# Silu in one ScalarE step for half of the gates, and the last tiles cut in column halves

## The chip, the cores and the metric

One core of a Trainium2 chip runs the kernel. The time is the device time of one execution in microseconds (us), and a median over several executions is quoted. Each execution also has a profiled span, from the first to the last instruction that the profile records. Ratios are computed as the mean time of one kernel's runs over that of the other's in the same rounds, so they are not quite the ratio of the quoted medians.

## The reference, cut to what matters

```python
x = A_x                                       # 2048 rows of 512
xn = _layernorm(x)
s = _A_ref(xn, A_wqkv, A_wo)                  # dilated local attention, then @ wo
g = _silu(_B_ref(xn, B_w1, B_w2, B_w3, B_w4)) # mixer and MLP: x1 + gelu(norm(x1) @ w3) @ w4
return x + s * g
```

The end of the kernel is `x + s * silu(x1 + h2)`: for each tile of 128 rows, the last MLP product (w4), the gate, the output projection (wo), a product, an add and a store.

## The kernel before: the parts that matter

Rows are split by parity: p is 0 for even rows and 1 for odd ones, with eight tiles each. Tiles t = 8 to 15 of the MLP are those of parity 1. `final_tile(p, i)` makes output tile i of parity p.

```python
    def w4_tile(t):
        ...
        def half(lo, hi):                       # lo..hi: part of the 11 steps of the contraction
            if lo == 0:
                st["pt"] = psb("w4_ps")
            pt = st["pt"]
            for ft in range(lo, hi):            # L521: TensorE
                nc.tensor.matmul(pt, lhsT=h3(c, ft, 1)[...], rhs=w4_sb[:fs, ft, :], ...)
            if hi == NF:
                x_i = xn[p][:, i, :]            # L527: VectorE
                nc.vector.tensor_tensor(out=x_i, in0=pt, in1=x_i, op=ALU.add)

    def gate(t):                                # x_i becomes 2 * silu(x_i)
        ...
        nc.scalar.activation(sig, x_i, AF.Tanh, scale=0.5)                        # L536: ScalarE
        nc.vector.scalar_tensor_tensor(out=x_i, in0=sig, scalar=1.0, in1=x_i,
                                       op0=ALU.add, op1=ALU.mult)                 # L537: VectorE

    def final_tile(p, i, eng=nc.vector, ps=psb, act=False):
        ...                                     # L683: four matmuls with wo
        if act:
            nc.scalar.copy(out=sg, in_=pt)                                        # L690
        nc.vector.tensor_tensor(out=sg, in0=sg if act else pt, in1=xn[p][:, i, :], op=ALU.mult)  # L691
        eng.tensor_tensor(out=x_o, in0=sg, in1=x_o, op=ALU.add)                   # L693

    ...                                         # the end of the program:
    for t in range(8, 16):
        w4s[t](4 * (t == 8), NF)
        if t == 10:
            normalise_end(1, 1)
        if t == 13:
            normalise_end(1, 2)                 # L660, L665: needs the last reciprocal denominators
        if t < 15:
            p, i = fq.pop(0)                    # (0,6), (1,0), (1,1), ... (1,5)
            final_tile(p, i, ps=psa)
            gate(t)
            ...                                 # stores
        if t == 10:
            normalise_mid(1, 2)                 # the reciprocal, and its way out to memory
            normalise_rr(1, 2)                  # and back, broadcast
    final_tile(0, 7, ps=psa)
    store(nc.sync, 0, 7, 1)
    gate(15)
    final_tile(1, 6, ps=psa, act=True)
    store(nc.sync, 1, 6, 1)
    final_tile(1, 7, ps=psa)
    store(nc.scalar, 1, 7, 1)
```

The factor 2 in the gate is paid back by attention denominators that are doubled (a column of 2.0 in the values).

The softmax here doesn't subtract the row's maximum and nothing guards it: scores larger than these inputs give would overflow.

Of the kernel before, what the change touches and what calls it, by code (L numbers as in the profile page):

```python
# [8 lines left out]
AF = mybir.ActivationFunctionType  # L9
ALU = mybir.AluOpType  # L10
# [5 lines left out]
def kernel(  # L16
# [14 lines left out]
    nc = tc.nc  # L31
    P = 128
    S = 2048
    D = 512
# [4 lines left out]
    ND = D // P  # L39
    NF = (F + P - 1) // P  # L40
# [43 lines left out]
    def at(kb, n, m):  # L84
        ar, o = (arenas[0], int(kb * KB)) if kb < 170 else (arenas[1], int((kb - 176) * KB))
        return ar[:, o : o + n * m].rearrange("p (n m) -> p n m", n=n)

    xn = [at(8 * p, M // P, D) for p in range(2)]
# [15 lines left out]
    oT = [at(176, ND, M), at(B0 + 17, ND, X)]  # L104
# [4 lines left out]
    w4_sb = at(121.5, NF, D)  # L109
    wo_sb = at(62, ND, D)  # L110
    xo = [at(B0 + 25.5, M // P, D), at(67, M // P, D)]
# [12 lines left out]
    def psb(name):  # L124
        cnt["b"] += 1
        return pst("wb"[cnt["b"] % 2], name)[:, 0, :]

    wqkv_v = A_wqkv.rearrange("(dt q) n -> q dt n", q=P)
    for c in range(NCH):
        p, k = c // 2, c % 2  # L130
        n = 1 if c == 0 else 2
        for t0 in range(k * TPC, (k + 1) * TPC, n):
            nc.sync.dma_start(
                out=xn[p][:, t0 : t0 + n, :],
                in_=xv[p, t0 * P : (t0 + n) * P, :].rearrange("(i q) d -> q i d", q=P),
# [354 lines left out]
    def h3(c, ft, n):  # L490
        if c < 3:
            return h3T[c][:, ft : ft + n, :]
        return h3T_lo[:, ft : ft + n, :] if ft < 8 else h3T_hi[:, ft - 8 : ft - 8 + n, :]
# [16 lines left out]
    def w4_tile(t):  # L510
        c, jj = t // TPC, t % TPC
        p, i = c // 2, (c % 2) * TPC + jj
        st = {}

        def half(lo, hi):
            if lo == 0:
                st["pt"] = psb("w4_ps")
            pt = st["pt"]
            for ft in range(lo, hi):
                fs = P if ft < NF - 1 else FL  # L520
                nc.tensor.matmul(  # L521
                    pt, lhsT=h3(c, ft, 1)[:fs, 0, jj * P : (jj + 1) * P], rhs=w4_sb[:fs, ft, :],
                    start=(ft == 0), stop=(ft == NF - 1),
                )
            if hi == NF:
                x_i = xn[p][:, i, :]
                nc.vector.tensor_tensor(out=x_i, in0=pt, in1=x_i, op=ALU.add)  # L527

        return half

    def gate(t):
        c, jj = t // TPC, t % TPC
        p, i = c // 2, (c % 2) * TPC + jj
        x_i = xn[p][:, i, :]
        sig = fin.tile([P, D], BF16, name="sig", tag="f")
        nc.scalar.activation(sig, x_i, AF.Tanh, scale=0.5)  # L536
        nc.vector.scalar_tensor_tensor(out=x_i, in0=sig, scalar=1.0, in1=x_i, op0=ALU.add, op1=ALU.mult)  # L537
# [83 lines left out]
    def normalise_dn(p, r):  # L621
        n = H * runs[p][r][3] // P
        dn = small.tile([P, n], BF16, name="dn", tag="dn")
        nc.sync.dma_start(out=dn, in_=rrs[p, r][0].rearrange("h (a m) -> (h a) m", a=P // 8))
        rrs[p, r][0] = dn
# [11 lines left out]
    def normalise_mid(p, r):  # L637
        _, _, ra, rw = runs[p][r]
        n = H * rw // P
        dn, rden_d = rrs[p, r]  # L640
        rb = small.tile([P, n], BF16, name="rb", tag="rb")
        with nc.allow_low_precision("bf16 weights"):
            nc.vector.reciprocal(out=rb, in_=dn)
        nc.sync.dma_start(out=rden_d.rearrange("h (a m) -> (h a) m", a=P // 8), in_=rb)

    def normalise_rr(p, r):
        _, _, ra, rw = runs[p][r]
        dn, rden_d = rrs[p, r]
        if p == 0 and r:
            rr = orws[r % 2][:, 0 : ND * rw]  # L650
        else:
            rr = at(rr_at[r % 2] if p else B0 + 8, 1, ND * rw)[:, 0, :]
        nc.sync.dma_start(out=rr, in_=rden_d.unsqueeze(1).to_broadcast([8, DH, ND * rw]))
        rrs[p, r] = rr

    def normalise_end(p, r):
        _, _, ra, rw = runs[p][r]
        rr = rrs[p, r].rearrange("p (s q) -> p s q", s=ND)
        n = min(rw, M - ra)
        nc.vector.tensor_tensor(  # L660
            out=oT[p][:, :, ra : ra + n], in0=oT[p][:, :, ra : ra + n], in1=rr[:, :, 0:n], op=ALU.mult
        )
        if rw > n:
            a = M - DW + W
            nc.vector.tensor_tensor(  # L665
                out=oT[0][:, :, a:M], in0=oT[p][:, :, a + DW : X], in1=rr[:, :, a + DW - ra : rw], op=ALU.mult
            )
# [7 lines left out]
            in_=xv[p, 4 * k * P : (4 * k + 4) * P, :].rearrange("(i q) d -> q i d", q=P),  # L675
        )

    def final_tile(p, i, eng=nc.vector, ps=psb, act=False):
        pt = ps("wo_ps")
        if ps is psa:  # L680
            pt = pt[:, 0, :]
        for dt in range(ND):
            nc.tensor.matmul(  # L683
                pt, lhsT=oT[p][:, dt, i * P : (i + 1) * P], rhs=wo_sb[:, dt, :],
                start=(dt == 0), stop=(dt == ND - 1),
            )
        cnt["g"] += 1
        sg = at(sg_at[cnt["g"] % 3], 1, D)[:, 0, :]
        if act:
            nc.scalar.copy(out=sg, in_=pt)  # L690
        nc.vector.tensor_tensor(out=sg, in0=sg if act else pt, in1=xn[p][:, i, :], op=ALU.mult)  # L691
        x_o = xo[p][:, i, :]
        eng.tensor_tensor(out=x_o, in0=sg, in1=x_o, op=ALU.add)  # L693

    def store(q, p, i, n=2):
        q.dma_start(
            out=ov[p, i * P : (i + n) * P, :].rearrange("(i q) d -> q i d", q=P), in_=xo[p][:, i : i + n, :]
        )
# [118 lines left out]
    w4s = [w4_tile(t) for t in range(S // P)]  # L817
# [3 lines left out]
    for k in range(NU):  # L821
        a, b = groups[N1 + k]
        gates = [lambda t=t: gate(t) for t in ready]
        ready = fill.get(k, ())
        if ready:
            a += gates
            if len(ready) == 2:
                a.append(lambda t=ready[0]: w4s[t](0, NF))
                late[N1 + k].append(lambda t=ready[0]: gate(t))
                ready = ready[1:]  # L830
            t = ready[-1]
            a.append(lambda t=t: w4s[t](0, 6))
            b.append(lambda t=t: w4s[t](6, NF))
        else:
            i0, i1, i2 = rows_of[k]
            a.append(lambda i=i0: final_tile(0, i, nc.gpsimd))
            a.append(lambda i=i1: final_tile(0, i, nc.gpsimd))
            a += gates
            b.append(lambda i=i2: final_tile(0, i, nc.gpsimd))
# [77 lines left out]
    pack(1, 2)  # L917
    normalise_dn(1, 2)
    gate(7)
    for i in (0, 2, 4):  # L920
        store(nc.sync, 0, i)
    fq = [(0, 6)] + [(1, i) for i in range(6)]
    for t in range(8, 16):
        w4s[t](4 * (t == 8), NF)
        if t == 10:
            normalise_end(1, 1)
        if t == 13:
            normalise_end(1, 2)
        if t < 15:
            p, i = fq.pop(0)  # L930
            final_tile(p, i, ps=psa)
            gate(t)
            if p == 0:
                store(nc.sync, p, i, 1)
            elif i % 2:
                store(nc.sync, p, i - 1)
        if t == 10:
            normalise_mid(1, 2)
            normalise_rr(1, 2)
    final_tile(0, 7, ps=psa)  # L940
    store(nc.sync, 0, 7, 1)
    gate(15)
    final_tile(1, 6, ps=psa, act=True)
    store(nc.sync, 1, 6, 1)
    final_tile(1, 7, ps=psa)
    store(nc.scalar, 1, 7, 1)


# [28 lines left out]
```

## Time and profile before

| | before |
|---|---|
| time, median of 3 | 206.06 us |
| profiled span | 204.1 us |
| TensorE's last result | 199.11 us |
| VectorE's last add ends | 201.03 us |
| last store issued | 201.06 us |

The median and the profile come from different executions: the profiled one took 205.92 us. The prediction shows the lines behind the last three rows.

### The profile page before, as it was taken

How to read it: one execution, taken by the hardware profiler on the slowest of the kernel's cores; microseconds unless marked ns; L12 is line 12 of the kernel's file. 1: busy time of each engine (PE TensorE's matmuls, PEld its weight loads, DVE VectorE, ACT ScalarE, POOL GpSimd, SP SyncE). 2: the span in 40 equal slices, each digit the busy share in tenths (PEclk: the TensorE clock that was granted, in tenths of full speed). 3: DMA queues.
4: the chain of work that ended last, by engine and by line, in shares of the span. 5: the costliest groups of instructions: out<-in, count | busy, mean ns of one | idle time of the engine just before them, and what ended most of it. 6: DMA issues, size and time to landing. Idle time of an engine off the chain costs nothing.

```text
span 204.1 us, 4800 instructions
## 1 busy us (share of the span) xinstructions
PE 195.2 (96%) x1900; PEld 94.9 (47%) x1928; DVE 135.0 (66%) x256; ACT 131.5 (64%) x157; POOL 74.5 (37%) x149
## 2 busy tenths in 40 slices
PE   7899999999999999999999999999999999999990
PEld 2585445444444444444444444444555444444440
DVE  5788897626298988856930101288577968888693
ACT  2366768657988888896556657898788877212130
POOL 5889842100023095964691000003830590700000
PEclk9999999999999999999999999999999999999997
DMA  5992264577900089495798948794220241553312
GB/s 146 356 348 80 87 139 86 85 109 112 275 34 5 14 199 140 75 254 107 181 196 184 295 148 136 109 278 156 36 51 5 56 89 26 116 165 118 117 51 77
DMA packets 33197, 26.74 MB, mean 131 GB/s; under 512 B 14600, under 2 KB 31088, under 8 KB 33176
## 3 DMA queue, kind: packets, MB, share of 16 engines
q1 hardware_dynamic: 30984, 23.22, 44.8%
q0 software_dynamic: 2048, 3.09, 8.9%
q8 instruction: 15, 0.25, 0.5%
q10 hardware_dynamic: 144, 0.13, 0.2%
q14 instruction: 6, 0.05, 0.1%
HBM read 12.40 MB, written 4.98 MB: 85 GB/s over the span
## 4 chain that ended last, share of the span: by engine, by line
PE 71%; DVE 11%; DMA 9%; issue 3%; POOL 3%; ACT 2%; SPq 0%; DVEq 0%; POOLq 0%
PE w_ps L501 19%; PE w_ps L521 10%; PE v_ps L547 8%; PE s_ps L567 7%; PE w_ps L457 6%; PE qk_ps L401 5%; PE w_ps L434 5%; PE o_ps L590 4%; PE qk_ps L419 4%; DMA den_d<-orw 3%; PE wo_ps L683 3%; DMA arena<-rden_d 2%; DVE arena L537 2%; DMA rden_d<-rb 1%; DVE arena L691 1%
## 5 line engine op out<-in xcount | busy, mean ns | idle before, releaser
L572 ACT ACTIVATE arena<-s_ps 128x960 bf16<-128x960 f32 (+1 forms) x68 | 62.7, 975 | 13.7 <-PE s_ps L567 13.7
L521 PE MATMUL w_ps<-arena 128*128 128x512 bf16 (+1 forms) x156 | 38.5, 380 | 0.6 <-issue 0.2
L506 ACT ACTIVATE arena<-w_ps 128x1024 bf16<-128x1024 f32 x20 | 20.5, 1024 | 14.5 <-PE w_ps L501 13.1
L632 POOL DMA_DIRECT2D arena<-orw x48 | 25.0, 528 | 5.8 <-DVE orw L602 5.8
L501 PEld LDWEIGHTS <-arena 128*128 128x128 bf16 (+1 forms) x176 | 17.5, 100 | 20.5 <-issue 0.4
L521 PEld LDWEIGHTS <-arena 128*128 128x128 bf16 (+1 forms) x176 | 16.5, 98 | 19.5
L693 POOL TENSOR_TENSOR arena<-arena 128x512 bf16<-128x512 bf16 x6 | 7.7, 1302 | 44.4 <-DVE arena L691 44.4
L536 ACT ACTIVATE sig<-arena 128x512 bf16<-128x512 bf16 x16 | 10.1, 631 | 21.0 <-DVE arena L527 20.9
L551 DVE CAST v_aug<-v_ps 128x512 bf16<-128x512 f32 x17 | 11.7, 690 | 15.4 <-PE v_ps L547 15.3
L602 DVE CAST orw<-o_ps 128x960 bf16<-128x960 f32 (+1 forms) x17 | 19.7, 1156 | 3.1 <-PE o_ps L590 3.0
L401 PE MATMUL qk_ps<-arena 128*128 128x512 bf16 (+1 forms) x109 | 20.4, 332 | 0.5 <-ACT arena L321 0.3
L501 PE MATMUL w_ps<-arena 128*128 128x512 bf16 (+1 forms) x86 | 19.4, 379 | 0.2
L501 PE MATMUL w_ps<-arena,arena 128*128 128x512 bf16 (+1 forms) x86 | 19.1, 379 | 0.1
L547 PE MATMUL v_ps<-wv_sb,arena 128*128 128x512 bf16 x67 | 17.5, 380 | 0.1
L567 PEld LDWEIGHTS <-arena 32*128 32x128 bf16 x544 | 10.2, 92 | 14.8 <-issue 14.7
L567 PE MATMUL s_ps<-arena 32*128 32x120 bf16 (+1 forms) x544 | 16.1, 213 | 0.1
L527 DVE TENSOR_TENSOR arena<-w_ps,arena 128x512 bf16<-128x512 f32 x16 | 11.0, 686 | 7.9 <-PE w_ps L521 7.9
L273 POOL TENSOR_SCALAR l3r<-l3m 128x1 f32<-128x1 f32 (+1 forms) x10 | 2.4, 238 | 37.6 <-DVE l3m L282 37.6
L457 PE MATMUL w_ps<-arena 128*128 128x512 bf16 x63 | 15.2, 380 | 0.1
L660 DVE TENSOR_TENSOR arena<-arena,orw 128x1440 bf16<-128x1440 bf16 (+1 forms) x2 | 1.6, 783 | 19.8 <-DMA orw<-rden_d 19.8
L434 PE MATMUL w_ps<-arena 128*128 128x512 bf16 x63 | 14.6, 379 | 0.0
L401 PEld LDWEIGHTS <-arena 128*128 128x128 bf16 x112 | 10.6, 98 | 7.9 <-DMA arena<-in_A_wqkv_dram 0.8
(99 smaller groups left out, 273.4 us busy)
## 6 DMA issues: line engine op xcount, KB each, us to landing
x1n_dram<-arena SPq DMA_DIRECT2D x5, 512.0 KB, 3.0
arena<-in_A_x_dram SPq DMA_DIRECT2D x4, 512.0 KB, 6.1
arena<-in_A_x_dram SPq DMA_DIRECT2D x6, 256.0 KB, 6.6
out_dram<-arena SPq DMA_DIRECT2D x6, 256.0 KB, 3.6
arena<-in_B_w_dram SPq DMA_DIRECT2D x1, 1376.0 KB
arena<-in_B_w_dram SPq DMA_DIRECT2D x1, 1280.0 KB
arena<-arena SPq DMA_DIRECT2D x16, 72.0 KB, 2.6
arena<-arena SPq DMA_DIRECT2D x16, 68.0 KB, 4.0
```

Source lines behind the costliest of these rows:

```text
L401: nc.tensor.matmul(pt[:, b, hh * w : (hh + 1) * w], lhsT=wqk_sb[:, dt, nt * P : (nt + 1) * P], rhs=xnT[p][:, dt, k * CH + hh * w : k * CH ...
L434: nc.tensor.matmul(pt[:, b, :], lhsT=w1_sb[:, dt, g * P : (g + 1) * P], rhs=xn2T[c][:, dt, :], start=(dt == 0), stop=(dt == ND - 1),)
L457: nc.tensor.matmul(pt, lhsT=w2_src(p, g, m0), rhs=w2_sb[:, g, :], start=(g == 0), stop=(g == ND - 1))
L501: nc.tensor.matmul(pt[:fs, ft % 2, :], lhsT=w3_sb[:, dt, ft * P : ft * P + fs], rhs=x1nT[c][:, dt, :], start=(dt == 0), stop=(dt == ND - 1),)
L506: nc.scalar.activation(h3(c, 2 * a, 2), pt, AF.Gelu_apprx_tanh)
L521: nc.tensor.matmul(pt, lhsT=h3(c, ft, 1)[:fs, 0, jj * P : (jj + 1) * P], rhs=w4_sb[:fs, ft, :], start=(ft == 0), stop=(ft == NF - 1),)
L547: nc.tensor.matmul(vp[:nk, :], lhsT=xnT[p][:, dt, k0 : k0 + nk], rhs=wv_sb[:, dt, :], start=(dt == 0), stop=(dt == ND - 1),)
L551: nc.vector.tensor_copy(out=va[:nk, :, 0:DH], in_=vp[:nk, :].rearrange("p (h d) -> p h d", d=DH))
L567: nc.tensor.matmul(st[:nk, b, i * nq : (i + 1) * nq], lhsT=kT[e][r : r + 32, dt, k0 : k0 + nk], rhs=qT[e][r : r + 32, dt, q0 : q0 + nq], s ...
L572: nc.scalar.activation(prv[:nk, 2 * h : 2 * h + 2], st[:nk, :, 0 : 4 * nq], AF.Exp, scale=SCALE)
L602: nc.vector.tensor_copy(out=orw[p, r][:, :, :, q0 - ra : q0 - ra + nq], in_=op[:, :, 0 : 4 * nq].rearrange("p j (s q) -> p j s q", q=nq),)
L632: nc.gpsimd.dma_start(out=oT[p][DH * hh : DH * (hh + 1), :, ra : ra + rw], in_=orw[p, r][32 * cg : 32 * cg + DH, jj],)
```

## The change

Its intent is to take VectorE's load off the tail. The gates of parity 1 become one Silu on ScalarE, in place. The output product doubles what is now a plain silu. The last MLP tile is made in two column halves, one behind the final of (0,7) and one behind that of (1,6), so that its gate lies beside TensorE's work. The last output tile is made in two halves too.

```diff
-        def half(lo, hi):
+        def half(lo, hi, ds=slice(0, D)):           # all of pt, w4_sb and x_i cut to columns ds
...
-    def gate(t):
+    def gate(t, ds=slice(0, D)):
...
+        if p:
+            nc.scalar.activation(x_i, x_i, AF.Silu)
+            return
...
-        if act:
-            nc.scalar.copy(out=sg, in_=pt)
...
+        for lo in range(0, D, n):                   # n = D // halves; matmuls, product, add per half
+            if p:
+                nc.vector.scalar_tensor_tensor(
+                    out=sg[:, ds], in0=pt, scalar=2.0, in1=x_i[:, ds], op0=ALU.mult, op1=ALU.mult
+                )
...
     gate(7)
+    nc.scalar.preload_act_table_set("silu_and_others")
...
     final_tile(0, 7, ps=psa)
     store(nc.sync, 0, 7, 1)
-    gate(15)
-    final_tile(1, 6, ps=psa, act=True)
+    w4s[15](0, NF, halves[0])                       # was whole, ahead of the final of (0,7)
+    gate(15, halves[0])
+    final_tile(1, 6, ps=psa)
     store(nc.sync, 1, 6, 1)
-    final_tile(1, 7, ps=psa)
+    w4s[15](0, NF, halves[1])
+    gate(15, halves[1])
+    final_tile(1, 7, ps=psa, halves=2)
     store(nc.scalar, 1, 7, 1)
```

## The prediction

> **What bounds the kernel now.** I read the page first, then the chain of waits for the last 38 us, then VectorE and TensorE one by one in order of time, then a table of busy time by stretch. The page says TensorE is busy 96% of the span, so outside the tail only less TensorE work could help, and the change removes none.
>
> ```profile
> PE 195.2 (96%) x1900; PEld 94.9 (47%) x1928; DVE 135.0 (66%) x256; ACT 131.5 (64%) x157; POOL 74.5 (37%) x149
> ...
> PE 71%; DVE 11%; DMA 9%; issue 3%; POOL 3%; ACT 2%; SPq 0%; DVEq 0%; POOLq 0%
> ```
>
> The end is different. TensorE's last instructions in order of time (start, us, engine, line, operation):
>
> ```profile
> 193.98 1.89 PE L521 MATMUL w_ps<-arena 128*128 128x512 bf16 x8
> 195.71 0.81 PE L521 MATMUL w_ps<-arena,arena 128*128 128x512 bf16 x3
> 196.36 1.03 PE L683 MATMUL wo_ps<-arena,arena 128*128 128x512 bf16 x4
> 197.22 1.89 PE L683 MATMUL wo_ps<-arena 128*128 128x512 bf16 x8
> ```
>
> The reader sees the last MLP tile (L521, eleven matmuls), then the finals of (0,7), (1,6), (1,7), without a gap, the last result at 197.22 + 1.89 = 199.11. VectorE from there back:
>
> ```profile
> 190.08 0.69 DVE L527 TENSOR_TENSOR arena<-w_ps,arena 128x512 bf16<-128x512 f32 x1 [0.62 <-PE w_ps L521]
> 191.94 0.78 DVE L660 TENSOR_TENSOR arena<-arena,arena 128x1184 bf16<-128x1184 bf16 x1 [1.17 <-DMA arena<-rden_d]
> 192.63 0.27 DVE L665 TENSOR_TENSOR arena<-arena,arena 128x224 bf16<-128x224 bf16 x1
> ...
> 196.74 0.68 DVE L527 TENSOR_TENSOR arena<-w_ps,arena 128x512 bf16<-128x512 f32 x1
> 197.43 0.69 DVE L691 TENSOR_TENSOR arena<-wo_ps,arena 128x512 bf16<-128x512 f32 x1
> 198.15 0.43 DVE L693 TENSOR_TENSOR arena<-arena 128x512 bf16<-128x512 bf16 x1
> 198.49 0.68 DVE L537 SCALAR_TENSOR_TENSOR arena<-sig,arena 128x512 bf16<-128x512 bf16 x1
> 199.10 0.42 DVE L691 TENSOR_TENSOR arena<-arena 128x512 bf16<-128x512 bf16 x1
> 199.55 0.42 DVE L693 TENSOR_TENSOR arena<-arena 128x512 bf16<-128x512 bf16 x1
> 199.89 0.68 DVE L691 TENSOR_TENSOR arena<-wo_ps,arena 128x512 bf16<-128x512 f32 x1
> 200.61 0.42 DVE L693 TENSOR_TENSOR arena<-arena 128x512 bf16<-128x512 bf16 x1
> ```
>
> Up to 190.8 VectorE waits 0.5 to 0.6 us for TensorE in every tile (the bracket of the first line). At 190.77 it waits 1.17 us for a transfer, the reciprocal denominators. From 191.94 it never waits again: it is behind, and it ends at 201.03, 1.92 us after TensorE. The store is issued at 201.06 and the span ends at 204.1, a fixed 3.04 us. So only the 1.92 us between TensorE's and VectorE's ends can be won.
>
> **What the Trainium skill says.** "ScalarE: Activation LUTs", section "Table sets: the hidden batching unit", lists exp and tanh in one set, and "What ACT_TABLE_LOAD costs" gives 1283 ns for a load, with a drain 2.66 us, and the same time per element for every function. The trace agrees on the load: four of 1.28 us, none after 127.2 since exp and tanh share it; a drain is not seen (the ACTIVATE follows at 128.50, 0.01 us after the load):
>
> ```profile
> 127.21 1.28 ACT L572 ACT_TABLE_LOAD   x1
> 128.50 1.94 ACT L572 ACTIVATE arena<-s_ps 128x1024 bf16<-128x1024 f32 x2
> ```
>
> "TensorE: Matmul & The Clock Gate", section "Back-to-back issue gap", gives 518 cycles for 512 columns and 262 for 256, so halving columns should double the count at nearly no cost. The trace agrees: the chain has 16 matmuls of 256 columns in 1.75 us (0.109 each), and 49 of 512 in 10.74 (0.219). "VectorE: DVE Perf Modes", section "The perf-mode tier table", puts a bf16 tensor_tensor from SBUF at twice the rate of one with a PSUM operand; here 0.425 against 0.686 us. No table line there has scalar_tensor_tensor; the trace has 0.684 us for it even in bf16 from SBUF, so I take 0.69 for the new one that reads PSUM.
>
> **The change, part by part.**
> 1. Silu gates, tiles 8 to 15. Removed from VectorE: eight L537 of 0.68 us, which cost 0.60 each from start to start, 4.8 us in all. On ScalarE a Tanh of 0.63 becomes a Silu of 0.63 (estimate: same width, same engine). The product of L691 becomes a scalar_tensor_tensor of the same length (the factor 2 balances the doubled denominators). For tiles 8 to 13 the 4.8 us are not on the path: VectorE only waits longer for TensorE. Only the gates of 14 and 15, in the backlog, count.
> 2. One table load more, after gate 7. ScalarE ends that Tanh at 172.20 and gets the next gate at 174.71: 2.51 us idle. 1.28 us fits; 2.66 would just about fit too, and Silu 8 is first used by the product at 178.0. Cost 0.
> 3. Gate 10 leaves VectorE ahead of the reciprocal (183.44), which feeds the denominators. The stage's transfers can start up to 0.6 us earlier, and L660 with them, at 191.4 instead of 191.94.
> 4. Order at the end of TensorE: before, tile 15 then (0,7), (1,6), (1,7). After: (0,7), half of 15, (1,6), other half of 15, (1,7) in two halves. The order of instructions of the built program confirms it. The columns are the same: PE still ends at about 199.1, plus 0.03 us for 30 matmuls more.
> 5. The copy of (1,6) on ScalarE (0.59) goes, and its product reads PSUM: +0.26 us of VectorE (0.68 for 0.42).
> 6. Halves on VectorE. Estimates of 256 columns: casts of 512 and 960 columns from PSUM take 0.690 and 1.148, so 1.02 ns a column and 0.17 fixed, hence 0.43; bf16 adds of 224 and 512 take 0.27 and 0.425, hence 0.285; Silu from ACT copies of 128, 512 and 1024 (0.27, 0.59, 1.02), 0.83 ns a column, hence 0.42.
>
> Walk through the new tail, with 0.04 us from producer to consumer and 0.08 overlap between independent VectorE instructions, both as in the lines above. TensorE results: (1,5) 194.15, (0,7) 195.01, 15 first half 196.20, (1,6) 197.07, 15 second half 198.25, (1,7) halves 198.69 and 199.15. VectorE: L660 191.4, L665 to 192.3, product and add of (1,4) to 193.4, tile 14 to 194.06, (1,5) to 195.3, (0,7) to 196.4, tile 15 first half to 196.74; here it has caught up and waits for (1,6): 197.11 to 198.25; second half 198.29 to 198.71; Silu on ScalarE 198.80 to 199.22; (1,7) first product 198.73 to 199.15, its add to 199.46, second product 199.40 to 199.82, its add to 200.12. So VectorE ends at about 200.15 in place of 201.03: **0.9 us** won, 206.06 - 0.9 = 205.2. A check of the sum: the same instructions packed without waits lose two gates (1.2), gain 0.26 and four small extra starts of about 0.15; the rest of the backlog goes into waits for TensorE.
>
> **The rivals.**
> (a) All 4.8 us are won (about 201.3). Against it: the 0.5 to 0.6 us waits for TensorE in front of L527 in each tile, and PE at 3.24 us per tile with no gap. It cannot be, unless TensorE got faster.
> (b) The Silu becomes the last wait: it stands between L527 and the last product. My slack is 0.2 us at the last half, 2 us and more at others. If the small ops cost 0.2 more each, 205.5.
> (c) The denominators come late all the same, since stores of (1,0) are queued in front of the write (the table by stretch shows the transfer engines 56% busy at 180 to 187). Then L660 begins at 191.9, VectorE catches up only at (1,6); the end is the same within 0.1. If it came 0.4 us later than before, TensorE's (1,5), which starts at 193.12 with L660 ending at 192.72, would be held, and the time would be 205.5 to 206.
> (d) The table load is placed badly or drains long, holding gate 8: nothing waits before 178.0, so 205.2 still.
>
> **Range and chances.** The ceiling of gain: last TensorE result 199.15, then a half product and a half add, 0.04 + 0.43 + 0.04 + 0.285, gives 199.95, a gain of 1.1; to this the runs' own spread of 0.3. The floor: rival (b) or (c), a gain of 0.3. So 204.7 to 205.9, and 205.2 in the middle. 2% is 4.1 us, twice what lies after TensorE's end; so within 2% is all but certain, 0.98; faster 0.01, slower 0.01.
>
> **What will show it.** Right: VectorE waiting for TensorE (not for a transfer or nothing) at (1,6) near 197.1; VectorE's last add ending near 200.1, TensorE's last result near 199.15, end 3.04 us after; one table load after 172.2 with ScalarE idle around it; VectorE busy about 4.7 us less on the page (8 x 0.684 removed, 0.26 for part 5 and some 0.49 for the halves added). Wrong: a TensorE gap in the last 10 us, a Silu longer than 0.63, products from PSUM longer than 0.69, 256-column instructions that don't shrink to 0.43 and 0.285, or a wait for the Silu in front of the last product. Had TensorE's end moved by more than 0.1 us, my whole sum would be off.

## The result, and the profile after

The changed kernel took 205.78 us (median of 6, 205.69 to 205.89) against 206.13 us for the kernel before (median of 6), a ratio of 0.9982 with a 95% interval of 0.9969 to 0.9995. The gain is 0.35 us, less than half of the 0.9 that was forecast.

The profile shows a gain twice as large. (In the lines, `w_ps` and `wo_ps` are the PSUM tiles that TensorE writes for w4 and wo, `arena` is the large on-chip tile in which the kernel lays out most of its data, and `rden_d` is the memory buffer through which the reciprocal denominators go.) This is the first line of the changed kernel's page; before it read 204.1 us.

```profile
span 203.4 us, 4821 instructions
```

VectorE in order of time in the changed kernel (start, us, engine, line, operation, and in brackets the idle time and what ended it):

```profile
190.23 0.69 DVE L527 TENSOR_TENSOR arena<-w_ps,arena 128x512 bf16<-128x512 f32 x1 [1.16 <-PE w_ps L521]
192.24 0.78 DVE L663 TENSOR_TENSOR arena<-arena,arena 128x1184 bf16<-128x1184 bf16 x1 [1.32 <-DMA arena<-rden_d]
...
196.90 0.42 DVE L527 TENSOR_TENSOR arena<-w_ps,arena 128x256 bf16<-128x256 f32 x1
197.34 0.69 DVE L696 SCALAR_TENSOR_TENSOR arena<-wo_ps,arena 128x512 bf16<-128x512 f32 x1
198.07 0.42 DVE L701 TENSOR_TENSOR arena<-arena 128x512 bf16<-128x512 bf16 x1
198.48 0.42 DVE L527 TENSOR_TENSOR arena<-w_ps,arena 128x256 bf16<-128x256 f32 x1
198.99 0.42 DVE L696 SCALAR_TENSOR_TENSOR arena<-wo_ps,arena 128x256 bf16<-128x256 f32 x1
199.44 0.29 DVE L701 TENSOR_TENSOR arena<-arena 128x256 bf16<-128x256 bf16 x1
199.65 0.42 DVE L696 SCALAR_TENSOR_TENSOR arena<-wo_ps,arena 128x256 bf16<-128x256 f32 x1
200.10 0.29 DVE L701 TENSOR_TENSOR arena<-arena 128x256 bf16<-128x256 bf16 x1
```

Three things are to be seen. In the middle tiles VectorE's idle time in front of L527 has nearly doubled, from 0.62 to 1.16 us: there the removed gates bought nothing. L663 (L660 before) still waits for the denominators, longer than before (1.32 us against 1.17). And the last add ends at 200.39, where it ended at 201.03. This trace also starts its work later: the same matmul of the tail stands at 172.53, before at 172.37, because the first input landed 0.16 us later (VectorE's first statistics start at 2.97, before at 2.81). Without that, VectorE's tail is 0.80 us shorter.

TensorE and ScalarE in the changed kernel:

```profile
197.94 0.49 PE L521 MATMUL w_ps<-arena,arena 128*128 128x256 bf16 x3
198.28 1.04 PE L691 MATMUL wo_ps<-arena 128*128 128x256 bf16 x8
```

```profile
172.38 1.28 ACT L928 ACT_TABLE_LOAD   x1
174.81 0.63 ACT L536 ACTIVATE arena<-arena 128x512 bf16<-128x512 bf16 x1 [1.15 <-DVE arena L527]
...
198.94 0.42 ACT L536 ACTIVATE arena<-arena 128x256 bf16<-128x256 bf16 x1 [1.17 <-DVE arena L527]
```

TensorE's last result is at 199.32, or 199.16 without the late start: it did not move. The load of the Silu table lies in ScalarE's idle time, with 1.15 us to spare before gate 8.

So a span gain of 0.7 us became a time gain of 0.35. What lies outside the profiled span (time minus span) grew. In the changed kernel's six executions it is 2.29 to 2.49 us; in the kernel before, in 37 executions run beside the experiments, it is 1.82 to 1.91. Even in the single executions that were profiled it is 205.82 - 203.4 = 2.42 against 205.92 - 204.1 = 1.82.

### The profile page after: what moved, and what is told of

It reads as the page before. It is cut to its first block, busy times and chain, and to the rows that moved or that the text cites. A ratio compares the mean times of both kernels' runs of the same rounds, so it can differ in the third digit from the quotient of the medians.

```text
span 203.4 us, 4821 instructions
## 1 busy us (share of the span) xinstructions
PE 194.9 (96%) x1915; PEld 96.1 (47%) x1943; DVE 131.2 (64%) x251; ACT 132.4 (65%) x158; POOL 74.3 (37%) x149
## 4 chain that ended last, share of the span: by engine, by line
PE 71%; DVE 10%; DMA 7%; POOL 4%; issue 3%; ACT 2%; DVEq 0%; POOLq 0%
PE w_ps L501 19%; PE w_ps L521 10%; PE v_ps L550 8%; PE s_ps L570 7%; PE w_ps L457 6%; PE qk_ps L401 5%; PE w_ps L434 5%; PE o_ps L593 4%; PE qk_ps L419 4%; PE wo_ps L691 3%; DMA arena<-rden_d 2%; DMA arena<-orw 2%; DVE arena L696 2%; DMA rden_d<-rb 2%; POOL arena L635 1%
## 5 line engine op out<-in xcount | busy, mean ns | idle before, releaser
L521 PE MATMUL w_ps<-arena 128*128 128x512 bf16 (+2 forms) x164 | 38.7, 370 | 0.5 <-issue 0.2
L501 PEld LDWEIGHTS <-arena 128*128 128x128 bf16 (+1 forms) x176 | 17.5, 100 | 20.6 <-issue 0.4
L521 PEld LDWEIGHTS <-arena 128*128 128x128 bf16 (+1 forms) x187 | 17.5, 98 | 19.0
L501 PE MATMUL w_ps<-arena 128*128 128x512 bf16 (+1 forms) x86 | 19.4, 379 | 0.2
L536 ACT ACTIVATE arena<-arena 128x512 bf16<-128x512 bf16 (+1 forms) x9 | 5.2, 582 | 20.4 <-DVE arena L527 20.4
L527 DVE TENSOR_TENSOR arena<-w_ps,arena 128x512 bf16<-128x512 f32 (+1 forms) x17 | 11.2, 659 | 10.8 <-PE w_ps L521 10.8
L663 DVE TENSOR_TENSOR arena<-arena,orw 128x1440 bf16<-128x1440 bf16 (+1 forms) x2 | 1.6, 783 | 19.3 <-DMA orw<-rden_d 19.3
```

The lines of the kernel that those rows point to most:

```text
L501: nc.tensor.matmul(pt[:fs, ft % 2, :], lhsT=w3_sb[:, dt, ft * P : ft * P + fs], rhs=x1nT[c][:, dt, :], start=(dt == 0), stop=(dt == ND - 1),)
L521: nc.tensor.matmul(pt, lhsT=h3(c, ft, 1)[:fs, 0, jj * P : (jj + 1) * P], rhs=w4_sb[:fs, ft, ds], start=(ft == 0), stop=(ft == NF - 1),)
```

## The experiments

Below, "outside" is time minus span, as a mean over a kernel's executions. Spans are given to 0.1 us. Spans are medians over the executions of one kernel.

### First: is it the third table set, the load, or chance?

The changed kernel needs a third set of ScalarE tables. The first theory was that this set costs something outside the span in every execution. The rivals were the load instruction itself, the longer TensorE stream, and chance. (The expectations speak of 30 more TensorE instruction pairs. The pages count 15 more matmuls and as many weight loads, 30 instructions in all.)

The control is the changed kernel itself.

> The changed kernel once more, to have it beside the others on one chip and with five rounds. Both theories expect what was seen: about 205.75 us, some 0.35 under the kernel before, with a profiled span near 203.3 to 203.5 (before: 204.1). The part of the time that lies outside the profiled span was 1.82 us for the kernel before and 2.42 for this one; if that difference is chance, this run and the fresh kernel before should differ by the full 0.7 to 0.9.

Next, the changed kernel without the third set, with a wrong result (relative error 0.44):

```diff
-            nc.scalar.activation(x_i, x_i, AF.Silu)
+            nc.scalar.activation(x_i, x_i, AF.Tanh)
-    nc.scalar.preload_act_table_set("silu_and_others")
```

> The changed kernel with its Silu steps run as Tanh and without the third table set (wrong result on purpose): same instructions on every engine, same lengths, one table load and one table set fewer. Theory T1 (a third distinct table set costs about 0.5 us outside the profiled span, each execution): about 205.2 us, 0.9 under before, span still about 203.4. Rival T2 (the set has nothing to do with it: the 30 more TensorE instruction pairs, or chance): about 205.75, as the control. Rival T3 (the load instruction at 172 us itself costs, not the set): 205.2 too, so the next two runs are needed.

Then the kernel before, with a load of a new set, or of one it uses anyway:

```diff
     gate(7)
+    nc.scalar.preload_act_table_set("silu_and_others")              # e1_before_silu_set
+    nc.scalar.preload_act_table_set("gelu_apprx_tanh_and_others")   # e1_before_gelu_reload
```

> The kernel before with one more table load of a set it does not otherwise use (that of Silu, which has Tanh too), after gate 7; gates stay Tanh with the VectorE step. T1: 206.6 us, 0.5 above before, span unchanged at 204.1. T2: 206.1, as before. T3 (the load itself): 206.6.

> The kernel before with one more table load at the same place, but of the Gelu set, which it already uses (and which has Tanh): as many load instructions as the run above, no third set. T1: 206.1 us, as before. T2: 206.1. T3: 206.6, the same as with the Silu set.

| run | time | span | outside |
|---|---|---|---|
| before, beside them (9 runs) | 206.05 | 204.2 | 1.86 |
| control | 205.88 | 203.5 | 2.45 |
| Tanh only | 205.79 | 203.3 | 2.49 |
| before, Silu set loaded | 206.11 | 204.2 | 1.89 |
| before, Gelu set loaded again | 206.11 | 204.2 | 1.89 |

The table theory falls, both for the set and for the load. Without the set the outside part stays long; with it in the kernel before it stays short. Chance falls too: the outside part keeps to within some 0.1 us of its mean inside a kernel, and there are two groups, near 1.87 and near 2.45. The control gained only 0.03% here, with an interval of 0.9984 to 1.0009.

### Second: the parts one at a time, TensorE's stream, and a floor

Two suspects were left that the changed kernel and its Tanh variant share: the 30 more TensorE instructions (15 matmuls with their weight loads), or a measured time that has a floor and does not follow the vector tail. Two runs also separate the parts of the change. The first is the Silu gates alone, with the old order and the old ScalarE copy of (1,6):

```diff
+        if p:                                        # in gate
+            nc.scalar.activation(x_i, x_i, AF.Silu)
+            return
...                                                   # in final_tile: the product doubled if p; load after gate 7
```

> Part 1 alone: Silu gates of parity 1 in the kernel before, TensorE's order and instructions as before (no halves). By my tail sum VectorE ends near 200.6 on the clock of the trace before, so the span should be 203.6 to 203.8. Theory T2 (the 0.55 us that appear outside the profiled span belong to the 30 more TensorE instructions): outside part stays 1.85, so 205.5 to 205.6 us, faster than the changed kernel. Theory T5 (the measured time has a floor near 205.8 that does not follow the end of the vector tail): 205.8 to 205.9.

The second is the changed kernel with nothing cut in halves:

```diff
-    w4s[15](0, NF, halves[0])
-    gate(15, halves[0])
+    w4s[15](0, NF)
+    gate(15)
     final_tile(1, 6, ps=psa)
     store(nc.sync, 1, 6, 1)
-    w4s[15](0, NF, halves[1])
-    gate(15, halves[1])
-    final_tile(1, 7, ps=psa, halves=2)
+    final_tile(1, 7, ps=psa)
```

> The changed kernel without halves: tile 15 whole, after the final of (0,7), then the finals of (1,6) and (1,7) whole. As many TensorE instructions as before. Tail sum: tile 15 added at 198.1, last product 199.4 to 200.1, last add to 200.5, so a span near 203.7. T2: outside part 1.85, 205.5 us. T5: 205.8.

The third is the kernel before with its warming matmuls cut in two; the fourth is the changed kernel with an idle product in front of the last add:

```diff
+            for hh in range(2):                      # in warm(): two matmuls of 256 columns for one of 512
```

> The kernel before with its 12 warming matmuls cut into 24 of half width (TensorE has 24 more instructions, same columns, all in the wait for the first input). T2: span 204.1, time 206.5, outside part 2.3 or more. T5: 206.1, outside part 1.85 as before.

```diff
+            if halves == 2 and lo:                   # in final_tile; idle is a scratch tile
+                nc.vector.scalar_tensor_tensor(out=idle, in0=x_i, scalar=2.0, in1=x_i, op0=ALU.mult, op1=ALU.mult)
             eng.tensor_tensor(out=x_o[:, ds], in0=sg[:, ds], in1=x_o[:, ds], op=ALU.add)
```

> The changed kernel with one idle VectorE product of 512 columns (0.6 us from start to start) put in front of the last add. The span must grow by 0.6 to 204.0. T2: the outside part stays 2.4 to 2.6, so 206.4 us. T5 (floor): the time stays near 205.85 and the outside part falls back to 1.85.

| run | time | span | outside |
|---|---|---|---|
| before, beside them (11 runs) | 206.12 | 204.3 | 1.87 |
| Silu alone | 206.09 | 204.3 | 1.78 |
| order, whole tiles | 205.57 | 203.8 | 1.80 |
| before, 12 more matmuls | 206.06 | 204.2 | 1.87 |
| changed, last add late | 205.72 | 203.9 | 1.78 |

The TensorE theory falls twice: 12 more matmuls in the kernel before cost nothing, and the late variant has all matmuls of the changed kernel and a short outside part. (The expectation of the third run speaks of 24 more instructions. A matmul and its weight load count as two here.)

The late variant is the odd one. It does 0.6 us more at the very end, its span grew by 0.5, and its time did not grow at all. That fits a floor, but the Tanh variant does not: two of its executions had a span of 202.9 and times of 205.36 and 205.45, so the time does follow the span down. What the late variant also has is one more instruction in VectorE's stream.

The parts of the span gain can be read too. Silu alone gains nothing (204.3), where 203.6 to 203.8 was expected. VectorE's and ScalarE's tail of a later run with the same tail, the one with 316 VectorE instructions below, shows why:

```profile
196.76 0.69 DVE L527 TENSOR_TENSOR arena<-w_ps,arena 128x512 bf16<-128x512 f32 x1 [0.70 <-PE w_ps L521]
...
199.10 0.69 DVE L696 SCALAR_TENSOR_TENSOR arena<-arena 128x512 bf16<-128x512 bf16 x1 [0.33 <-ACT arena L693]
...
200.89 0.43 DVE L702 TENSOR_TENSOR arena<-arena 128x512 bf16<-128x512 bf16 x1
```

```profile
198.49 0.59 ACT L693 CAST arena<-wo_ps 128x512 bf16<-128x512 f32 x1 [0.37 <-PE wo_ps L686]
```

VectorE is no longer behind: it waits 0.70 us for tile 15. But then it waits for the ScalarE copy of (1,6), which had been hidden behind its backlog, and it ends where it did. The new order without the copy gives 0.5 us of span (203.8 against 204.3); how much of that is the order and how much the copy, no run separates. The halves give 0.3 to 0.4 more (the changed kernel's runs have 203.4 and 203.5).

One execution of the whole-tile kernel, the profiled one, took 206.31 us where the other five took 205.52 to 205.66. Its TensorE and VectorE:

```profile
194.03 1.04 PE L691 MATMUL wo_ps<-arena 128*128 128x512 bf16 x4 [0.59 <-DVE arena L663]
```

```profile
193.20 0.78 DVE L663 TENSOR_TENSOR arena<-arena,arena 128x1184 bf16<-128x1184 bf16 x1 [2.27 <-DMA arena<-rden_d]
```

The denominators came late, and L663 with them: at 193.20, where the other profiles, of every kernel, have it at 191.41 to 192.69. The final of (1,5) on TensorE waited 0.59 us. This is the case of the prediction's third rival in which TensorE is held. No other profile shows it.

### Third: is it the layout of VectorE's stream?

Theory L says that the extra 0.6 us hang on the number of instructions in VectorE's stream. Theory E says that they hang on when its tail ends. The three variants have one idle VectorE product more than the changed kernel. One stands in the slack of tile 11; one stands where the late variant has it, but is cut to 32 columns; one stands after the last add, where nothing waits for it.

```diff
+        if t == 11:                                  # e3_idle_early, after final_tile(p, i, ps=psa)
+            nc.vector.scalar_tensor_tensor(out=idle, in0=xn[0][:, 0, :], scalar=2.0, in1=xn[0][:, 0, :], ...)
...
+                nc.vector.scalar_tensor_tensor(out=idle[:, 0:32], in0=x_i[:, 0:32], ...)    # e3_idle_short
...
     final_tile(1, 7, ps=psa, halves=2)
+    nc.vector.scalar_tensor_tensor(out=idle, in0=xn[0][:, 0, :], ...)                       # e3_idle_end
```

> The changed kernel again, on the chip of the three runs beside it. In all 16 runs so far (its own 11 and the 5 of the Tanh variant) time minus profiled span was 2.3 to 2.6 us; the kernel before and every other variant had 1.7 to 1.9. If that belongs to the kernel and not to the chip, it is 2.3 to 2.6 here too: about 205.85 us at a span of 203.4.

> The changed kernel with one idle VectorE product of 512 columns in tile 11's slack, some 15 us ahead of the end: span as the control's, 203.4. Theory L (the extra 0.6 us outside the span hang on how the instruction stream lies, since one more VectorE instruction in the late variant took them away): outside part 1.8, so 205.2 us. Theory E (they hang on when the vector tail ends): 2.4, so 205.85.

> The idle product of the late variant cut to 32 columns: the instruction stream is laid out exactly as there, but the last add is only some 0.15 to 0.2 us later than in the changed kernel, span 203.6. Theory L: outside part 1.8, 205.4 us. Theory E: 2.2 to 2.4, near 205.85.

> The idle product of 512 columns after the last add instead: the store is issued as in the changed kernel, VectorE works 0.7 us longer while the store flies, span 203.4. Theory L: 1.8 outside, 205.2 us. Theory E (the store's time counts): 2.4, 205.85; if VectorE's own end counts, 1.8.

| run | time | span | outside | ratio to before |
|---|---|---|---|---|
| before, beside them (7 runs) | 206.14 | 204.3 | 1.86 | |
| control (the changed kernel) | 205.99 | 203.5 | 2.49 | 0.9994 |
| idle product early | 205.35 | 203.6 | 1.79 | 0.9965 |
| idle product short | 205.20 | 203.4 | 1.80 | 0.9958 |
| idle product at the end | 205.25 | 203.4 | 1.83 | 0.9954 |

Theory L holds and E falls. The kernels do the same work in the same profiled span, and one useless instruction, in each of the three places tried, is worth 0.6 to 0.8 us of time. The page of the run with the idle product at the end begins

```profile
span 203.3 us, 4850 instructions
```

and the page of the control beside it reads 203.5 us and 4849 instructions, so the profile shows the added product but not where the 0.7 us went. (The 4821 on the changed kernel's first page is lower because 28 matmul records are missing there: PE x1915 for x1943.) This version beats both kernels: its interval against the kernel before is 0.994 to 0.9969, and it is 0.7 us under the control of the same chip.

### Fourth: does VectorE's count alone decide, and which counts?

Counted in the built programs, VectorE's stream has 318 instructions in the kernel before, 316 in the changed one and its Tanh variant, 317 in all variants with one idle product, 312 with whole tiles and 310 with Silu alone. (A recount of the built programs gives two fewer for every kernel; the steps between them are the same.) The last runs put other counts into other kernels, by idle products of 32 columns in tile 11:

```diff
+        if t == 11:
+            for _ in range(n):          # whole tiles: n = 1, 2, 3, 4; changed: 4; Silu alone: 6
+                nc.vector.tensor_tensor(out=idle, in0=xn[0][:, 0, 0:32], in1=xn[0][:, 0, 0:32], op=ALU.mult)
```

> The whole-tile variant (312 VectorE instructions in the built program, outside part 1.79 us) with three idle VectorE products of 32 columns in tile 11's slack: 315. If only the number 316 (the changed kernel's) is bad: outside part 1.8, time 205.5 to 205.7 at a span of 203.8. If a stretch up to 316 is bad, 2.4, time 206.2.

> The same with four idle products: 316, with TensorE's and ScalarE's instructions unlike the changed kernel's (3897 and 245 against 3927 and 246). If VectorE's number of instructions alone decides, outside part 2.4, time 206.2 at a span of 203.8; if the halves on TensorE are needed too, 1.8 and 205.6.

> The changed kernel with four idle products: 320 VectorE instructions. If one instruction more was enough because 316 is a single bad place: outside part 1.8, 205.2 to 205.3 us at a span of 203.4. If every fourth number is bad: 2.4, 205.85.

> The Silu gates alone (310 VectorE instructions, outside part 1.78) with six idle products: 316, ScalarE 246 as in the changed kernel, TensorE 3897. If VectorE's number alone decides: outside part 2.4, about 206.7 us at a span of 204.3. If not: 1.8 and 206.1.

> The whole-tile variant with one idle product: 313 VectorE instructions. 312 had 1.79 us outside the span, 315 and 316 had 2.4. If the bad stretch is four counts wide (313 to 316): 2.4 outside, 206.2 us. If it starts later: 1.8, 205.6.

> The same with two idle products: 314. Four wide: 2.4 outside, 206.2 us; a pair (315 and 316): 1.8, 205.6.

| VectorE instructions | kernels (executions) | time | outside |
|---|---|---|---|
| 310 | Silu alone (5) | 206.09 | 1.78 |
| 312 | whole tiles (6) | 205.57 | 1.80 |
| 313 | whole tiles (2) | 205.55 | 1.80 |
| 314 | whole tiles (2) | 205.97 | 1.97 and 2.48 |
| 315 | whole tiles (4) | 206.23 | 2.47 |
| 316 | whole tiles (4) | 206.19 | 2.51 |
| 316 | Silu alone (4) | 206.63 | 2.33 |
| 316 | changed (15, in three sets) | 205.78 to 205.99 | 2.44 |
| 317 | changed, one idle product (17) | 205.20 to 205.72 | 1.78 to 1.83 |
| 318 | before (37) | 206.05 to 206.15 | 1.86 |
| 320 | changed, four idle products (4) | 205.36 | 1.96 |

In these three kernels VectorE's count decides. The whole-tile kernel and the kernel with Silu alone were good; at 316 both lose 0.55 to 0.7 us outside the span, with spans of 203.8 and 204.3 that did not move and with TensorE streams unlike the changed kernel's. Counts of 315 and 316 are bad; at 314 one of two executions was bad; 310, 312, 313, 317 and 318 are good, and 320 nearly so (1.87 to 2.07). ScalarE's count doesn't decide: the Tanh variant and the whole-tile kernel both have 245 instructions there, with 2.49 and 1.80 us outside. Not tested are the kernel before at 315 or 316, and whether it is the count as such or a place in memory that moves with it.

What happens in those 0.6 us is not in the profile, so their mechanism stays open. The Trainium skill, page "Runtime: NRT & Kernel Launch", section "Instruction fetch mechanics", says that an engine's instructions are fetched in blocks of 256 and that a taken branch to a target outside the loaded blocks stalls on a fetch. In the built program each engine's main stream ends in a branch to a short closing block, and 0.6 us that come and go with a count of instructions would fit such a stall. But 314 to 316 lie near no multiple of 256 as counted, how many instructions stand in front of them on the chip isn't on record, and no run here shows a fetch. So this is an argument and not a finding.

## Why the prediction was wrong, point by point

**The step that failed** is the one that turns a span into a time. In the prediction's words: "So VectorE ends at about 200.15 in place of 201.03: **0.9 us** won, 206.06 - 0.9 = 205.2." The subtraction takes it for granted that what lies outside the profiled span (1.82 us in the profiled execution) stays as it is. It grew by 0.58 us (2.44 against 1.86, means of 15 and 37 executions), because the change left VectorE with 316 instructions; why that number costs time stays open. With one instruction more the same kernel took 205.20 to 205.35 us, and that is where the prediction put it. That 205.78 still lies between 204.7 and 205.9 is luck: the slow end was set for rivals (b) and (c), and what cost the time was neither, nor anything else that a rival named. The other steps:

- **The tail sum held.** VectorE's last add was forecast for 200.12; it came at 200.39, or 200.23 without the late start. The gain was 0.80 us for the 0.9 of the walk. (The prediction's check of its sum gives less: 1.2 - 0.26 - 0.15 = 0.79.) The last store still took 3.0 us to the end (200.39 to 203.4). The small rest shows first at the first half product: it starts 0.09 us after the end of the add in front of it, where 0.02 was reckoned; its cause was not tested.
- **The idle time in the middle tiles** grew from 0.62 to 1.16 us, so rival (a), all 4.8 us won, failed for the reason given. VectorE's busy time on the page fell by 3.8 us (135.0 to 131.2) and not by 4.7: the forecast took 0.684 us for each gate, though the prediction itself counts 0.60 from start to start. With 0.60 the sum is 4.8 - 0.26 - 0.49 = 4.05; the rest is open.
- **The table load** cost nothing: 1.28 us, then 1.15 us of idle time before gate 8, so rival (d) did not come. Loaded in the kernel before, it moved neither span nor time.
- **Part 3 was wrong, rival (c) right.** The reciprocal did start earlier, and so did the write of the denominators. These are the reciprocal, the issue of the write and that of the read back, first before the change, then after it:

```profile
183.44 0.71 DVE L643 RECIPROCAL rb<-dn 128x90 bf16<-128x90 bf16 x1
184.17 0.70 SPq L644 DMA_DIRECT2D rden_d<-rb  x1
187.18 0.61 SPq L653 DMA_DIRECT2D arena<-rden_d  x1
```

```profile
183.00 0.71 DVE L646 RECIPROCAL rb<-dn 128x90 bf16<-128x90 bf16 x1
183.73 0.34 SPq L647 DMA_DIRECT2D rden_d<-rb  x1
187.11 0.61 SPq L656 DMA_DIRECT2D arena<-rden_d  x1
```

  But the write took 3.36 us to land where it had taken 2.99, the read back 5.01 where it had taken 4.63, and L663 started at 192.24, not 191.4. That queued stores are the reason, as rival (c) says, was not tested. VectorE caught up only at (1,6): its product starts at 197.34, 0.10 us after TensorE's result at 197.24. The forecast wait there shows as no idle time in the profile, and the end hardly moved.
- **The small operations** were 0.42 and 0.29 us for 0.43 and 0.285, Silu 0.63 and 0.42 as estimated, and a product from PSUM 0.69. TensorE's end did not move, though the prediction counts 30 matmuls more; there are 15 (x1943 weight loads on the page for x1928).
- **Rival (b)** did not come: the last Silu ends at 199.36, the last product starts at 199.65.
- **Not foreseen among the parts**: that Silu alone would bring nothing, since the ScalarE copy becomes the last wait. The change removes that copy, so the sum was not harmed.

## What to carry to other kernels

Gains of less than one microsecond should be checked in two numbers, the time and the profiled span: if they move by different amounts, the loss lies outside what the profile records, and no wait in it will explain that. Before a small change is judged, one idle instruction in the slack of an engine whose instruction count has changed is a cheap test; here it was worth more than the change. And work taken off an engine pays only where that engine ends last: of 4.8 us of gates removed, 0.8 us reached the span, and only after the wait for the ScalarE copy behind them was removed and TensorE's order changed too.

## What the Trainium skill lacked or had wrong

- "Runtime: NRT & Kernel Launch" (section "The ~15µs preamble/postamble breakdown") calls the gap between a profile's total and the runtime's time kernel-invariant. That is another pair of quantities, so the runs don't contradict it, but no page found says more of such a gap. The one between time and profiled span was not invariant here: 1.86 us for the kernel before, 2.44 for the changed one, 1.83 for the changed one with an idle instruction at its end.
- The same page (section "Instruction fetch mechanics") calls the cost of crossing a fetch block "mostly hidden". If the fetch is what the counts of 315 and 316 meet, which no run shows, it was 0.6 us here. No page says that the number of instructions in an engine's stream can matter to the time.
- "VectorE: DVE Perf Modes" (section "The perf-mode tier table") has no row for scalar_tensor_tensor. Here 512 columns took 0.684 us from bf16 in SBUF and 0.685 with one operand in PSUM.
- "ScalarE: Activation LUTs" (section "What ACT_TABLE_LOAD costs") counts a drain of 1.38 us with every switch to a different set. The traces show 1.28 us loads, and an ACTIVATE 0.01 us after one of them in the kernel before; no drain appears.
